# PSUM as eight one-bank tiles instead of three two-bank and two one-bank tiles, with sums of products taken bank by bank

## The chip, the core and the metric

One core of a Trainium2 chip. The metric is device time in microseconds (us) of one execution. A core has a matrix engine (PE; its weight loads are listed apart as PEld), three engines for elementwise work (DVE, ACT, POOL) and a queue that issues most transfers (SP). Each works through its own instruction list in order, and they hand results to one another by semaphores. PSUM, into which PE writes its products, has eight banks of 512 fp32 columns on 128 partitions; DVE and ACT read it, POOL and the transfers don't.

## The reference

Attention with a band mask over q, k, v of 8 batches x 8 heads x 576 positions x 64, half of the heads with a plain window of 32 and half with a dilated one; then a Fourier mixing, a normalisation and a two-layer perceptron with a residual:

```python
scores = scale * np.matmul(q, k.transpose(0, 1, 3, 2))
scores = np.where(masks[None, :, :, :], scores, -1000000000.0)
attn = softmax(scores)                       # max, exp, sum, divide
x = (attn @ v) as (B, S, C)                  # C = 512
u = x + real(fft(fft(x, axis=1), axis=2))
un = (u - mean(u)) / sqrt(var(u) + 1e-6)
out = u + maximum(un @ w_ch1, 0.0) @ w_ch2   # 512 -> 2048 -> 512
```

## The kernel before

**Order.** No engine's list is written by hand. Each step is registered with `add(engine, cost, function, reads, writes, priority)`, and `Plan.run` (L238) places the steps on the engines by a list schedule over assumed costs, such as `dve(n)` (L354); the instructions are then emitted in that order, and the waits between engines are generated from what each instruction reads and writes. The planner knows its buffers by tag: a step that first touches a new buffer of a tag is placed only once the buffer that many slots back has been given up (`place`, L256). So the order is fixed before the program runs; the semaphores only hold an engine back at a place in its list.

**PSUM.** Three tiles `duo0` to `duo2` of 1024 columns (two banks each) and two tiles of one bank, `ff0` and `ff1` (L396 to L401). The halves of the duos serve different steps: both halves of `duo0` are the pair `sc` (scores), the halves of `duo1` are `pt` and `av`, those of `duo2` are the two slots of `mix`. In the last stage each duo is used whole, as an accumulator of 1024 columns.

**Attention** (L518 to L630, until about 509 us). 96 steps; in each, PE writes scores into a half of each bank of `sc` (L547), DVE adds the mask and takes the minimum (L556), ACT exponentiates (L562), PE transposes into `pt` (L575), ACT copies that out as `ptsb` (L578), PE multiplies with v into `av` (L582), and DVE reads `av` for the sums, the reciprocal and the scaled output `xt` (L590 to L594), which SP stores.

**Mixing** (L683 to L859), one batch after another beside attention: POOL, DVE and ACT fold the rows; PE transforms along the sequence (L764, L786) into the slots of `mix`, ACT and DVE copy that out in two parts (`y`, L769 and L770; `ye`, L791 and L792); PE transforms along the channels (L810, L816), again into `mix`, and ACT (`pc`, L820) and DVE (`dm`, `sq`, L824 and L826) read it. Then come normalisation and a store.

**Fills** (L1103 to L1127). Six of the sixteen feature blocks of the perceptron are done beside and behind mixing, in 18 fills of 256 tokens. A fill has six *ups* (L944: 12 matmuls of 256 columns into one bank, then ACT L950 and DVE L952 read that bank, one after the other) and, for each of two tiles, a *down* of 18 matmuls of 512 columns (L960) that ACT copies out as `row` (L980). Thirteen fills use `ff0` and `ff1` in turn; the five *late* ones use `pt` and `av` in turn for the ups and the halves of `sc` for the downs (L1105, L1110, L1114). Beside them weights for the last stage are loaded into the two buffers `wst` and prepared by ACT, DVE and POOL.

**Last stage** (L1197 to L1295, from about 752 us): nine chunks of 512 tokens, the other ten feature blocks. `late_up` (L1205) uses `ff`; `late_down` (L1241) computes seven products per pair of blocks into two accumulators, `ab` and `cd`, each a duo; POOL, ACT and DVE build the operands (L900, L902, L1223 to L1227). After the last pair `finish_two` (L1014) adds both accumulators to rows in SBUF with six DVE instructions (L1034), multiplies and adds once per tile (L1045), and stores. It is called 18 times.

Of the kernel before, what the change touches and what calls it, by code (L numbers as in the profile page):

```python
# [9 lines left out]
F32 = mybir.dt.float32  # L10
# [5 lines left out]
ALU = mybir.AluOpType  # L16

B, H, S, D = 8, 8, 576, 64
C, FF = 512, 2048
P = 128  # L20
# [5 lines left out]
TOK1 = 2 * P  # L26
# [153 lines left out]
class Plan:  # L180
# [21 lines left out]
    def add(self, eng, cost, fn, r=(), w=(), prio=0.0, nbytes=0, at=0.0):  # L202
        op = Op()
        op.eng, op.cost, op.fn, op.prio, op.nbytes = eng, cost, fn, prio, nbytes
        op.num, op.after, op.ready, op.start = len(self.ops), [], at, None
        self.ops.append(op)
        deps, bufs = set(), {}
        for items, writes in ((r, False), (w, True)):
            for it in items:
                b, key = it if isinstance(it, tuple) else (it, None)  # L210
                bufs[id(b)] = b
                keys = set(b.writer) | set(b.readers) if key is None else {key, None}
                for x in keys:
                    if x in b.writer:
                        deps.add(b.writer[x])
                    if writes:
                        deps.update(b.readers.get(x, ()))
        for items, writes in ((r, False), (w, True)):
            for it in items:
                b, key = it if isinstance(it, tuple) else (it, None)  # L220
                if writes:
                    if key is None:
                        b.writer, b.readers = {None: op.num}, {}
                    else:
                        b.writer[key] = op.num
                        b.readers.pop(key, None)
                else:
                    b.readers.setdefault(key, []).append(op.num)
        op.bufs = list(bufs.values())
        for b in op.bufs:  # L230
            b.left += 1
        deps.discard(op.num)
        op.waits = len(deps)
        for d in deps:
            self.ops[d].after.append(op)
        return op
# [109 lines left out]
def pe(n, m=P):  # L346
    return max(n / 2400 + 0.0025, m / 1200)
# [6 lines left out]
def dve(n):  # L354
    return n * 0.00104 + 0.07
# [17 lines left out]
def fused_kernel(ctx: ExitStack, tc, q, k, v, w1, w2, seq, tail, chn, alt, mask, ident, perm, flip, out):  # L373
    nc = tc.nc
    plan = Plan()
    add = plan.add
# [11 lines left out]
    pools = {}  # L388
# [4 lines left out]
    pools["mix"] = keep = mix_ctx.enter_context(tc.tile_pool(name="mix", bufs=1))  # L393
    pools["att"] = heads = att_ctx.enter_context(tc.tile_pool(name="att", bufs=1, side="right"))

    duos = [pools["psum"].tile([P, 1024], F32, name=f"duo{i}") for i in range(3)]  # L396
    zs = [pools["psum"].tile([P, 512], F32, name=f"ff{i}") for i in range(2)]
    pair, (pt_bank, av_bank), mixes = [[d[:, :512], d[:, 512:]] for d in duos]
    views = {"sc": pair, "pt": [pt_bank], "av": [av_bank], "mix": mixes, "ff": zs}
    views.update({f"duo{i}": [d] for i, d in enumerate(duos)})  # L400
    plan.behind.update({"sc": ("half",), "duo0": ("sc", "half"), "duo1": ("pt", "av"), "duo2": ("mix",)})  # L401

    def halves():
# [8 lines left out]
    def ring(tag, of):  # L412
        b = Buf(None, tag)
        plan.slots[tag] = len(of)
        line = plan.tags.setdefault(tag, [])
        ap = of[len(line) % len(of)]
        b.make = lambda: ap
        line.append(b)
        return b

    def bank(tag):
        return ring(tag, views[tag])
# [13 lines left out]
    def utb(i=0):  # L436
        return ffnb("ut", [P, 2, KT, TOK1], F32R, NUT)
# [33 lines left out]
    def dma(fn, r, w, prio, nbytes, slow=1):  # L471
        return add("SP", 0.5, fn, r, w, prio, nbytes * slow)
# [390 lines left out]
    def flat(t, lo, n, dtype=F32):  # L863
        return t().rearrange("p i k t -> p (i k t)")[:, lo:lo + n].bitcast(dtype)
# [118 lines left out]
    def read_u(idx, dst, key, prio):  # L983
        if order(idx) == 0:
            dma(lambda: nc.sync.dma_start(out=dst(), in_=u_rows(idx)), ((us[idx // 4], idx % 4),), (key,), prio, P * 2056)
        else:
            kk = order(idx) - 1
            add("POOL", 1.04, lambda: nc.gpsimd.indirect_dma_start(
                dst(), None, us[idx // 4](), bass.IndirectOffsetOnAxis(ap=flip_sb()[:, 4 * kk + idx % 4:4 * kk + idx % 4 + 1], axis=0)),
                ((us[idx // 4], idx % 4), flip_sb), (key,), prio, P * 2056)  # L990
        add("ACT", act(C), lambda: nc.scalar.activation(
            out=dst()[:, 0:C], in_=dst()[:, 0:C], func=AF.Identity, bias=dst()[:, C:C + 1], scale=1.0), (), (key,), prio)

    def write_out(idx, row, done, prio):
        if idx >= NREST:
            pair_ = idx - NREST
            queues = ((nc.sync, "SP"), (nc.scalar, "ACT"))
            for n in range(4):
                e, side = divmod(n, 2)

                def put(e=e, side=side):
                    lo = 256 + 33 * side
                    p0 = 64 * e + 32 * side
                    queues[e][0].dma_start(out=out[2 * pair_ + e, lo:lo + 32], in_=row()[p0:p0 + 32])
                add(queues[e][1], 0.5, put, (done,), (), prio, 32 * 2048)
            return
        for b, lo, p0, n in out_rows(idx):
            dma(lambda b=b, lo=lo, p0=p0, n=n: nc.sync.dma_start(
                out=out[b, lo:lo + n], in_=row()[p0:p0 + n]), (done,), (), prio, n * 2048)

    def blocks(x):
        return x.rearrange("p (n c) -> p n c", c=TOK1)

    def finish_two(idx, ab, cd, prio):  # L1014

        f1, f2 = utb(), utb()
        uks = [(f2, ("u", e)) for e in range(2)]

        def u(e):
            return flat(f2, (C + 2) * e, C + 2)  # L1020

        def part():
            return flat(f1, 0, 2 * C)

        for e in range(2):
            read_u(idx + e, lambda e=e: u(e), uks[e], prio)
            dma(lambda e=e: nc.sync.dma_start(out=part()[:, C * e:C * e + C], in_=parts[idx + e]()),
                (parts[idx + e],), ((f1, ("p", e)),), prio, P * 2048)
        ps = ((f1, ("p", 0)), (f1, ("p", 1)))
        soon = min(prio, SOON)  # L1030
        outer, inner = slice(0, 4, 3), slice(1, 3)

        def take(at, x, need, op=ALU.add):
            add("DVE", dve(C), lambda: nc.vector.tensor_tensor(  # L1034
                out=blocks(part())[:, at], in0=blocks(part())[:, at], in1=x(), op=op), need, ps, soon)
        take(outer, lambda: blocks(ab())[:, 3::-3], (ab,))
        take(inner, lambda: blocks(ab())[:, 0:2], (ab,))
        take(outer, lambda: blocks(ab())[:, 2:0:-1], (ab,), ALU.subtract)
        take(inner, lambda: blocks(ab())[:, 2:4], (ab,))
        take(outer, lambda: blocks(cd())[:, 2:4], ((cd, 1),))  # L1040
        take(outer, lambda: blocks(cd())[:, 0:1].broadcast_to([P, 2, TOK1]), ((cd, 0),))
        for e in range(2):
            def row(e=e):
                return part()[:, C * e:C * e + C]
            add("DVE", dve(C), lambda e=e, row=row: nc.vector.scalar_tensor_tensor(  # L1045
                row(), row(), u(e)[:, C + 1:C + 2], u(e)[:, 0:C], op0=ALU.mult, op1=ALU.add), (uks[e],), (ps[e],), soon)
            write_out(idx + e, row, ps[e], prio)
# [43 lines left out]
    def load_ut(c, gate, prio):  # L1091
        raw, tr = utb(), utb()
        ut = ring("utl", utviews)
        tokens(c, 0, 4, (raw, lambda: words(raw)), (tr, lambda: words(tr)), ut, 1, "POOL", (gate,), min(prio, SOON))
        return ut
# [47 lines left out]
    w2s = [Buf() for _ in range(NPAIR)]  # L1143
# [91 lines left out]
    def late_down(p, hl, accs2, prio):  # L1235
        for n, (i, j, which, block, opens) in enumerate(PRODUCTS):
            acc = accs2[which]

            def go(i=i, j=j, block=block, opens=opens, acc=acc):
                for n, (a, x) in enumerate(PASSES):  # L1240
                    nc.tensor.matmul(  # L1241
                        acc()[:, TOK1 * block:TOK1 * block + TOK1], lhsT=hl()[:, a, i], rhs=w2s[p]()[:, j, x],
                        start=(opens and p == 0 and n == 0), stop=(p == NPAIR - 1 and n == 2), skip_group_check=True,
                    )
            key = (hl, ("raw" if i < 2 else "sum", 0)), (hl, ("raw" if i < 2 else "sum", 1))
            add("PE", 3 * pe(TOK1), go, (*key, w2s[p]), ((acc, block // 2),), prio + 0.001 * n)
# [76 lines left out]
```

## Time and profile before

| | |
|---|---|
| three timed runs | 1256.28, 1256.88, 1265.43 us (median 1256.88) |
| the profiled execution | 1251.71 us, of which the span from the first to the last instruction is 1249.9 us |
| PE busy | 1133.9 us (91%) |
| PEld busy | 984.5 us (79%) |
| DVE, ACT, POOL busy | 743.2, 524.6, 518.0 us |
| mean granted clock of PE | 0.981 of full |

In the rows below an engine's idle time stands in brackets or behind a bar with what ended it (`<-ACT low L950`: an instruction of ACT at line 950 that wrote `low`). Matmuls overlap and their ends are modelled, so a stall looks longer on PEld, whose loads are short, than on PE; the two are views of one stall and are not added. In the names of the trace `duo` stands for any of the three duos.

### The profile page before, as it was taken

Reading aid. Unit: us, or ns where it says so; the run is one execution under the profiler, and the core shown is the slowest. Engines: PE = TensorE matmul, PEld = TensorE weight load, DVE = VectorE, ACT = ScalarE, POOL = GpSimd, SP = SyncE. Lnnn points to the kernel's source line nnn. Section 1 sums busy time; section 2 is a strip of 40 time slices with the busy share of each in tenths; the row PEclk is TensorE's granted clock in tenths of the full one; section 3 lists DMA queues with packets and bytes.
Section 4 is the critical chain, followed back from the end, with each engine's and each line's share of the span. In section 5 each row is a group of like instructions: output and inputs, shape, how many; then the busy total and the mean of one; then the engine's idle time right before and its main releaser. Section 6 shows DMA issues by size and latency. Waiting matters only on the chain.

```text
span 1249.9 us, 21610 instructions
## 1 busy us (share of the span) xinstructions
PE 1133.9 (91%) x7750; PEld 984.5 (79%) x7750; DVE 743.2 (59%) x2141; ACT 524.6 (42%) x1282; POOL 518.0 (41%) x636
## 2 busy tenths in 40 slices
PE   8998878889889888989987779999999999999996
PEld 7886767677778777868866668888898988889886
DVE  6577857665556654778645324547384654738446
ACT  5456635544544543343423114433334343343432
POOL 2034534434224221563321115737456373655644
PEclk9899989999798999999999999999999999999999
DMA  9464527444435431524423222222240422314121
GB/s 318 151 199 158 176 62 210 129 149 123 138 106 168 119 111 54 155 85 144 135 84 101 51 72 81 59 78 68 77 126 19 118 68 68 86 59 127 34 86 34
DMA packets 103805, 137.14 MB, mean 110 GB/s; under 512 B 9145, under 2 KB 61817, under 8 KB 103697
## 3 DMA queue, kind: packets, MB, share of 16 engines
q1 hardware_dynamic: 100128, 126.85, 34.2%
q0 software_dynamic: 3040, 8.09, 2.2%
q8 instruction: 61, 1.00, 0.3%
q10 hardware_dynamic: 528, 0.82, 0.2%
q14 instruction: 48, 0.39, 0.1%
HBM read 97.92 MB, written 37.80 MB: 109 GB/s over the span
## 4 chain that ended last, share of the span: by engine, by line
PE 55%; DVE 7%; ACT 4%; issue 3%; POOL 1%; DVEq 0%; ACTq 0%; POOLq 0%
PE ff L1205 19%; PE duo L1241 15%; PE ff L944 5%; PE ff L960 4%; PE duo L944 4%; PE duo L960 2%; DVE low L902 2%; ACT low L1084 2%; PE duo L810 1%; PE duo L582 1%; PE duo L547 1%; DVE low L952 1%; ACT low L950 1%; PE duo L764 1%; PE duo L575 1%
## 5 line engine op out<-in xcount | busy, mean ns | idle before, releaser
L1205 PE MATMUL ff<-low,wb 128*128 128x512 f32 x1080 | 263.5, 394 | 0.0
L1205 PEld LDWEIGHTS ff<-low,wb 128*128 128x128 f32 x1080 | 197.2, 188 | 42.2 <-POOL low L1087 3.4
L562 ACT ACTIVATE pm<-pm,mx 96x128 f32<-96x128 f32 x384 | 131.9, 394 | 74.3 <-DVE mx L556 73.1
L1241 PE MATMUL duo<-w2s,low 128*128 128x256 f32 x1134 | 148.9, 283 | 5.0 <-DVE low L902 5.0
L1241 PEld LDWEIGHTS duo<-w2s,low 128*128 128x128 f32 x1134 | 143.9, 190 | 11.6 <-DVE low L902 7.2
L902 DVE TENSOR_TENSOR low<-y,low 128x640 fp32r<-128x640 f32 x90 | 86.7, 963 | 82.6 <-ACT low L900 82.6
L944 PE MATMUL ff<-ut,low 128*128 128x256 f32 x936 | 132.2, 292 | 2.3 <-DVE low L952 1.3
L900 ACT CAST low<-y 128x640 fp32r<-128x640 f32 x90 | 65.5, 728 | 157.2 <-POOL y L1227 119.2
L944 PEld LDWEIGHTS ff<-ut,low 128*128 128x128 f32 x936 | 120.3, 195 | 4.1 <-DVE low L952 1.7
L556 DVE CUSTOM_DVE_ANT_0 pm<-duo,mask_sb 96x128 f32<-96x128 f32 x384 | 92.7, 279 | 41.8 <-PE duo L547 40.9
L960 PE MATMUL ff<-low 128*128 128x512 f32 x468 | 112.9, 393 | 0.5 <-DVE low L952 0.5
L902 DVE TENSOR_TENSOR low<-xa,low 128x256 fp32r<-128x256 f32 x45 | 36.5, 810 | 119.7 <-ACT low L900 119.7
L1241 PE MATMUL duo<-low 128*128 128x256 f32 x756 | 98.7, 284 | 2.4 <-DVE low L902 2.3
L1241 PEld LDWEIGHTS duo<-low 128*128 128x128 f32 x756 | 94.7, 191 | 7.2 <-DVE low L902 5.0
L960 PEld LDWEIGHTS ff<-low 128*128 128x128 f32 x468 | 85.8, 188 | 17.4 <-DVE low L952 0.7
L582 PE MATMUL duo<-vt,ptsb 128*96 128x65 f32 x768 | 90.4, 259 | 9.0 <-DVE xt L594 5.1
L582 PEld LDWEIGHTS duo<-vt,ptsb 128*96 128x96 f32 x768 | 81.5, 174 | 19.6 <-DVE xt L594 9.7
L1223 POOL TENSOR_TENSOR y<-xa 128x256 f32<-128x256 f32 x45 | 33.3, 739 | 150.3 <-ACT xa L1211 144.8
L1211 ACT ACTIVATE xa<-ff 128x256 f32<-128x256 f32 x90 | 34.5, 384 | 124.2 <-PE ff L1205 120.9
L944 PE MATMUL duo<-ut,low 128*128 128x256 f32 x360 | 55.7, 294 | 24.5 <-DVE low L952 12.5
L1067 DVE STREAM_TRANSPOSE ut<-ut 128x512 f32<-128x512 f32 (+1 forms) x76 | 70.5, 968 | 11.2 <-DMA ut<-us 10.7
L547 PE MATMUL duo<-kb,tq 64*96 64x128 f32 x768 | 66.7, 302 | 7.8 <-DVE mx L556 7.3
(136 smaller groups left out, 1955.2 us busy)
## 6 DMA issues: line engine op xcount, KB each, us to landing
vt<-in_v_dram SPq DMA_DIRECT2D x32, 390.0 KB
wst<-in_w_dram SPq DMA_DIRECT2D x20, 512.0 KB
us<-uc SPq DMA_DIRECT2D x36, 257.0 KB
tq<-in_q_dram SPq DMA_DIRECT2D x32, 288.0 KB
part<-row SPq DMA_DIRECT2D x36, 256.0 KB
ut<-us SPq DMA_DIRECT2D x36, 256.0 KB
ut<-part SPq DMA_DIRECT2D x36, 256.0 KB
kb<-in_k_dram SPq DMA_DIRECT2D x31, 288.0 KB
```

The source lines that it names most:

```text
L547: nc.tensor.matmul(sc()[e][:QB, KB * n:KB * n + KB], lhsT=tq()[ps, QB * t:QB * t + QB], rhs=kb()[ps, QB * t:QB * t + KB], start=True, stop ...
L556: nc.vector.tensor_tensor_reduce(pm()[:, i], sc()[i % 2][:QB, KB * (i // 2):KB * (i // 2) + KB], mask_sb()[:, masks[blocks[i // 2]]], -0.1 ...
L562: add("ACT", 0.295, lambda i=i: nc.scalar.activation(out=pm()[:, i], in_=pm()[:, i], func=AF.Exp, bias=mx()[:, i:i + 1], scale=-1.0), ((mx ...
L582: add("PE", 0.16, lambda i=i: nc.tensor.matmul(av()[:QB, 65 * i:65 * i + 65], lhsT=pt()[:, i], rhs=vt()[:, i % 2, blocks[i // 2]], start=T ...
L900: add("ACT", act(n), lambda: nc.scalar.copy(out=dst(0), in_=src()), need, ((key[0], (key[1], 0)),), prio)
L902: add(eng, (pool if eng == "POOL" else dve)(n), lambda: lo.tensor_tensor(out=dst(1), in0=src(), in1=dst(0).bitcast(F32), op=ALU.subtract), ...
L944: nc.tensor.matmul(z()[:, :n_tok], lhsT=wf()[:, a, kk], rhs=ut()[:, p, kk], start=(kk == 0 and n == 0), stop=(kk == KT - 1 and n == 2),)
L960: nc.tensor.matmul(acc(), lhsT=h()[:, a, P * s:P * s + P], rhs=wf()[:, p], start=(first and n == 0), stop=(last and n == 2),)
L1067: nc.vector.transpose(out=o[back], in_=x[:, g])
L1205: nc.tensor.matmul(z(), lhsT=wb1[NF1 + 2 * p + f]()[:, a, kk], rhs=ut()[:, x, kk], start=(kk == 0 and n == 0), stop=(kk == KT - 1 and n == 2),
L1211: add("ACT", act(TOK1) - 0.05, lambda z=z, x=x, side=side, cols=cols: nc.scalar.activation(out=x()[:, cols], in_=z()[:, TOK1 * side:TOK1 * ...
L1241: nc.tensor.matmul(acc()[:, TOK1 * block:TOK1 * block + TOK1], lhsT=hl()[:, a, i], rhs=w2s[p]()[:, j, x], start=(opens and p == 0 and n == ...
```

## The change

Eight tiles `bank0` to `bank7` of one bank each take the place of the duos and of `ff`, in the same places. `sc`, `pt`, `av`, `mix` and `ff` name single banks as before. A buffer of a duo tag is now a list of two banks, made by a function (`callable(ap)`). `late_down` picks the bank by `block // 2`. In `finish_two` the four DVE instructions that read both halves of `ab` become six, three for each bank: one of 512 columns and two of 256; the two that read `cd` stay. The planner is told the smaller cost for the 256-column ones.

```diff
-    duos = [pools["psum"].tile([P, 1024], F32, name=f"duo{i}") for i in range(3)]
-    zs = [pools["psum"].tile([P, 512], F32, name=f"ff{i}") for i in range(2)]
-    pair, (pt_bank, av_bank), mixes = [[d[:, :512], d[:, 512:]] for d in duos]
-    views = {"sc": pair, "pt": [pt_bank], "av": [av_bank], "mix": mixes, "ff": zs}
-    views.update({f"duo{i}": [d] for i, d in enumerate(duos)})
+    eight = [pools["psum"].tile([P, 512], F32, name=f"bank{i}") for i in range(8)]
+    pair, pt_av, mixes, zs = [eight[i:i + 2] for i in range(0, 8, 2)]
+    views = {"sc": pair, "pt": pt_av[:1], "av": pt_av[1:], "mix": mixes, "ff": zs}
+    views.update({f"duo{i}": [lambda i=i: eight[2 * i:2 * i + 2]] for i in range(3)})
...
-        b.make = lambda: ap
+        b.make = ap if callable(ap) else lambda: ap
...
         def take(at, x, need, op=ALU.add):
-            add("DVE", dve(C), lambda: nc.vector.tensor_tensor(
+            add("DVE", dve(C if at in (outer, inner) else TOK1), lambda: nc.vector.tensor_tensor(
                 out=blocks(part())[:, at], in0=blocks(part())[:, at], in1=x(), op=op), need, ps, soon)
-        take(outer, lambda: blocks(ab())[:, 3::-3], (ab,))
-        take(inner, lambda: blocks(ab())[:, 0:2], (ab,))
-        take(outer, lambda: blocks(ab())[:, 2:0:-1], (ab,), ALU.subtract)
-        take(inner, lambda: blocks(ab())[:, 2:4], (ab,))
-        take(outer, lambda: blocks(cd())[:, 2:4], ((cd, 1),))
-        take(outer, lambda: blocks(cd())[:, 0:1].broadcast_to([P, 2, TOK1]), ((cd, 0),))
+        for n in range(2):
+            take(inner, lambda n=n: blocks(ab()[n]), ((ab, n),))
+            take(slice(3 * (1 - n), 3 * (1 - n) + 1), lambda n=n: blocks(ab()[n])[:, n:n + 1], ((ab, n),))
+            take(slice(3 * (1 - n), 3 * (1 - n) + 1), lambda n=n: blocks(ab()[n])[:, 1 - n:2 - n], ((ab, n),), ALU.subtract)
+        take(outer, lambda: blocks(cd()[1]), ((cd, 1),))
+        take(outer, lambda: blocks(cd()[0])[:, 0:1].broadcast_to([P, 2, TOK1]), ((cd, 0),))
...
-                        acc()[:, TOK1 * block:TOK1 * block + TOK1], lhsT=hl()[:, a, i], rhs=w2s[p]()[:, j, x],
+                        acc()[block // 2][:, TOK1 * (block % 2):TOK1 * (block % 2) + TOK1], lhsT=hl()[:, a, i], rhs=w2s[p]()[:, j, x],
```

## Rows read from the trace of the kernel before

**Rows 1.** The page, part 2: busy tenths of PE and its granted clock in 40 slices of 31.2 us.
```profile
PE   8998878889889888989987779999999999999996
...
PEclk9899989999798999999999999999999999999999
```
**Rows 2.** Busy time of the engines by stage: attention with mixing and the first fills, late fills, last stage, its end. Columns: stretch and its length, PE, PEld, DVE, ACT, POOL busy us with instructions, granted clock, DMA share, GB/s.
```profile
0.00:628.00 628.00, 555.41 (x4247) 478.31 (x4248) 411.94 (x1697) 299.67 (x783) 221.28 (x288) 0.96 0.48 144
628.00:752.00 124.00, 95.97 (x534) 77.58 (x533) 45.22 (x77) 29.61 (x62) 21.41 (x20) 1.00 0.28 80
752.00:1220.00 468.00, 462.80 (x2823) 410.25 (x2823) 266.71 (x340) 188.33 (x423) 260.56 (x310) 1.00 0.27 76
1220.00:1250.00 30.00, 19.68 (x151) 18.37 (x149) 19.33 (x28) 6.95 (x14) 14.71 (x18) 0.95 0.13 36
```
**Rows 3.** Waits of PEld from 0 to 628 us: who waited for whom, us in total, times, longest.
```profile
PEld duo L575 <- ACT pm L562: 13.8, 28, 1.2
PEld duo L547 <- DVE mx L556: 12.7, 24, 0.9
PEld duo L582 <- DVE xt L594: 9.7, 20, 1.6
PEld duo L575 <- DVE sums L590: 8.9, 18, 1.0
PEld duo L575 <- DVE xt L594: 8.8, 13, 1.2
PEld duo L810 <- ACT pc L820: 7.2, 15, 0.8
PEld duo L764 <- DVE y L770: 5.4, 6, 1.1
PEld duo L582 <- ACT ptsb L578: 5.0, 11, 0.8
PEld duo L786 <- DVE y L770: 4.8, 7, 1.0
...
PEld duo L764 <- ACT ye L791: 3.6, 5, 0.7
...
PEld duo L810 <- DVE dm L824: 2.5, 3, 0.9
PEld duo L764 <- ACT y L769: 2.4, 6, 0.5
PEld duo L816 <- DVE sq L826: 2.4, 3, 0.8
```
**Rows 4.** Waits of DVE and of ACT from 0 to 628 us, those between a reader of one half of `duo1` and a user of the other half.
```profile
DVE sums L590 <- PE duo L575: 18.0, 26, 2.6
...
DVE sums L590 <- ACT ptsb L578: 7.6, 13, 1.2
...
ACT ptsb L578 <- DVE sums L590: 18.6, 17, 4.0
...
ACT ptsb L578 <- PE duo L582: 8.6, 7, 2.6
```
**Rows 5.** The timeline in a late fill: start us, us, engine, line, operation, count, and the idle time before it with what ended it.
```profile
731.91 0.42 PEld L944 LDWEIGHTS duo<-ut,low 128*128 128x128 f32 x3 [0.68 <-ACT low L950]
...
732.64 0.42 DVE L952 SCALAR_TENSOR_TENSOR low<-duo,low 128x256 fp32r<-128x256 f32 x1 [2.58 <-PE duo L944]
733.12 1.13 PEld L944 LDWEIGHTS duo<-ut,low 128*128 128x128 f32 x9 [0.79 <-DVE low L952]
...
734.55 0.38 ACT L950 ACTIVATE low<-duo 128x256 fp32r<-128x256 f32 x1 [2.69 <-PE duo L944]
734.99 0.42 PEld L944 LDWEIGHTS duo<-ut,low 128*128 128x128 f32 x3 [0.74 <-ACT low L950]
```
**Rows 6.** Waits of PEld from 628 to 752 us, all there are.
```profile
PEld duo L944 <- ACT low L950: 17.2, 24, 1.2
PEld duo L944 <- DVE low L952: 17.0, 21, 1.2
PEld duo L960 <- ACT row L980: 5.6, 5, 1.1
```
**Rows 7.** PE's matmuls of the late fills by line, 628 to 752 us: count, busy us, mean ns, and idle us before them.
```profile
L944 PE MATMUL duo<-ut,low 128*128 128x256 f32 x354 | 54.6, 294 | 24.5 <-DVE low L952 12.5 <-ACT low L950 12.1
L960 PE MATMUL duo<-low 128*128 128x512 f32 x179 | 43.4, 394 | 3.5 <-ACT row L980 3.5
```
**Rows 8.** The chain of work that ended last, two pieces of a fill in `ff`: start us, us, what, matmuls.
```profile
613.88 2.84 PE ff L944 x24
...
619.97 8.17 PE ff L960 x36
```
**Rows 9.** The queue's own waits (SP) over the span: loads of `wst` behind POOL's preparation.
```profile
SPq L882 <- POOL wb L902: 34.8, 10, 6.0
```
**Rows 10.** A window of 6 us, with the columns of rows 2.
```profile
324.00:330.00 6.00, 5.35 (x33) 4.43 (x33) 2.74 (x19) 3.48 (x10) 0.00 (x0) 0.50 0.52 146
```
**Rows 11.** DVE's instructions that read a duo: duration ns min/median/max, first and last start us, shapes.
```profile
L1034 DVE TENSOR_TENSOR ut<-ut,duo x108: 672/679/691, 799.5 to 1243.9; 128x512 f32<-128x512 f32 x108
...
L824 DVE TENSOR_TENSOR dm<-pc,duo x24: 389/418/426, 110.7 to 576.4; 128x258 f32<-128x258 f32 x16, 33x258 f32<-33x258 f32 x8
```
**Rows 12.** Waits of PEld in the last stage, 752 to 1220 us, for DVE.
```profile
PEld duo L1241 <- DVE low L902: 9.4, 16, 0.7
```

## The prediction

> **What bounds the kernel now.** I read the busy line by slices first: PE is at 9 in every slice of the last 40% except the final one, and at 7 to 9 before that, so whatever this change gives must come from the first 750 us [rows 1]. The windows by stage say how much room there is: 72.6 us without PE work in the first 628 us (628 - 555.4), 28.0 in the late fills (124 - 96.0), 5.2 in the 468 us of the last stage [rows 2]. No other engine is full in the first two: DVE has 66% and 36%.
>
> Next, the waits, to see whom PE stalls for. In the late fills three rows hold all of it, 39.8 us on PEld [rows 6]. The timeline shows the pattern: PE starts an up in one half of `duo1` the moment ACT has read the *other* half, does three matmuls, stands still until DVE has read that other half too, then does nine. ACT and DVE in turn start only when PE has paused [rows 5]. These instructions share no column and no bank with one another, only the tile. The same in attention: DVE's `sums` reads `av` and waits 18.0 us for transposes into `pt`; ACT's `ptsb` reads `pt` and waits 18.6 us for `sums`; neither needs the other's data [rows 4]. So the generated waits order engines by tile, also a reader against a reader, and a tile of two banks ties two unrelated steps together.
>
> **Late fills.** The change makes `pt` and `av`, and the halves of `sc`, tiles of their own. All of [rows 6] is then without a cause: the up waits for the other bank, and the down of one tile (L960) for the copy of the other tile's bank. What it leaves can be read from the earlier fills, which do the same instructions on two one-bank tiles: 24 matmuls of an up in 2.84 us, 36 of a down in 8.17 us, that is 0.118 and 0.227 us each [rows 8]. The stage holds 354 and 179 of them [rows 7]: 354 x 0.118 + 179 x 0.227 = 82.5 us, against 124: a gain of 41.5. One up now takes 734.99 - 731.91 = 3.08 us [rows 5]; at the other rate it is 1.42, in which ACT (0.38) and DVE (0.42) can empty the other bank. From below: in the second and third late fill the weights are prepared too, and their loads already wait for POOL to free `wst` [rows 9]; DVE's list mixes that preparation with L952, so a late load holds L952, and behind it the next up but one. Those waits are 3.5 us each (34.8 / 10); if four loads are late by that and PE with them, the gain is 41.5 - 14 = 27.5. I take 36, nearer to the upper end, because [rows 6] gives 39.8 by another view, and DVE's work of this stage fits (45 us in what becomes 85 to 90).
>
> **The first 628 us.** I sort PEld's waits [rows 3] by what the instruction needs. Nine rows are waits for the reader of another bank: transposes into `pt` for readers of `av` (8.9 + 8.8), and the transforms in one slot of `mix` for readers of the other slot (7.2, 2.5, 5.4, 2.4, 3.6, 4.8, 2.4): 46.0 us. They lose their cause. Four rows are true: L575 needs the exponentials `pm` (13.8), L547 the half of `sc` that DVE reads (12.7), L582 the one bank `av` (9.7) and `ptsb` (5.0): 41.2 us. But three of these are late because ACT and DVE were themselves held by the other half [rows 4]: `sums`, and with it `xt`, by 25.6 us, `ptsb` by 27.2 us, and the exponentials behind `ptsb` in ACT's list.
>
> Of the 46.0 I take 70%, 32 us: where a false wait goes, the next true one on PE's fixed list comes nearer, and DVE, which will have 412 us of work in some 570 instead of 628, answers later. Of the 28.5 us for `pm`, `xt` and `ptsb` two thirds, 19. Of `mx` a quarter, 3: the change splits `sc` between its two banks, so DVE can start on the first bank one matmul earlier, but two steps still share each bank, in halves of 256 columns, and the new scores wait for the old. [...]
>
> [...] I take a fifth back, 5 us; bounds 0 and 25. Sum here: 32 + 19 + 3 + 5 = 59 us. Bounds: 15, a third of the 46.0 with nothing else, and 46 + 41 + 25 = 112, everything.
>
> **Last stage.** In each of 18 `finish_two` DVE has two instructions more: four of 512 columns at 0.679 us were 2.72; two of these and four of 256 at 0.418 (the nearest row, 258 columns read from PSUM) are 3.03 [rows 11]. That is 0.31 us each, 5.7 in all. The cover is DVE's idle time, 201 of the 468 us [rows 2]; PE's only waits for DVE here are for L902, 9.4 us in 16 [rows 12]. If every added 0.31 held L902, it would be 5.7 us. I take 0, and 0.3 for the last `finish_two`, behind which there is no work. `cd` can be read one product earlier, which the six takes of `ab` before it hide. The first `take` starts at 799.5 us [rows 11], so the planner, whose costs differ only there, places everything before as now. The views, the function in `ring` and the names add no instruction; no transfer is added or moved, and SP's stores and loads only follow their producers earlier.
>
> **Sum:** 36 + 59 - 0 = 95 us. The profiled execution took 1251.7 us, so 1157; the median of the runs is 5 above it, so 1162 by that. I say **1158 us**.
>
> **Rivals.**
> *The next wait takes over.* PE's list is fixed; a step freed from `av` may only stand until `pm` or the loads arrive. Then the first stage gives 15 and the late fills 27.5: 1256.9 - 42.5 = 1214. For it: DVE at 66%, and mixing is a chain over four engines. Against it: [rows 4] lie on that very chain.
> *Everything behind follows.* 41 and some 95 of the 112: 1256.9 - 136 = 1121. For it: the waits of ACT and DVE in [rows 4] sum to 53 us beside PE's own, and stalls shorter than a matmul's modelled end don't show. Against it: DVE would have to run at 412 of about 530 us. [...]
> *The waits don't go.* If the releasers named in [rows 4, 6] stood for other semaphores, nothing is released: 1257, no change. Against it: the pattern repeats with the same 0.68 and 0.79 us at every up.
> *Slower: the split sums.* DVE works in order; if the added 0.31 us stand ahead of L902 in each of 18 places, PE stands 5.7 us, and the end is 0.3 later: 1263. It decides only if the first two stages give less than 6 us. Against it: 57% DVE.
>
> **How the numbers follow.** Forecast (1130 to 1190) 0.60; next wait 0.17; everything follows 0.16; no release 0.04; split sums 0.03. A change under 1%, 12.6 us, can't be told from none in this kernel. The first three cases are faster by more than that, 0.93; the fourth and a third of the fifth lie within 1%, 0.05; slower by more 0.02, where the split sums cost more than reckoned. The range takes in the forecast and most of both neighbours: 1112 to 1208.
>
> **What would show it.** Right: from the late fills L944 and L960 at 0.118 and 0.227 us each, the stage near 85 to 90 us, and no wait of PE for L950 within an up; in attention no wait of `sums` for L575 nor of `ptsb` for `sums`; more DVE share in the first stage; the 468 us of the last stage unchanged. Wrong in size: waits of L575 for `pm` or of L952 for transfers that grow by as much as the others fall. Wrong in kind: the pairs of [rows 4] still there between different banks.

## The result and the profile after

The changed kernel takes **1138.34 us** (median of 4 runs, 1136.03 to 1143.46); the kernel before, run beside it, 1256.58. The ratio is 0.9063, with a 95% interval of 0.8995 to 0.9131. The forecast was 1158 us, with a range of 1112 to 1208.

Medians and means below leave out the runs that took over 1.5% longer than the fastest of their kernel: two of E1's ten (1266.73 and 1269.13 us), one of E8's six (1495.78) and one of the eleven of the kernel before that ran beside E5 to E8 (1611.23).

The profiled execution of the changed kernel is the slowest of its four, 1143.46 us, and that of before was 5 us faster than its median. So the traces show 108.2 us of the 118. The page's head and the slices of PE answer to [rows 1]; line numbers from L547 on are one lower than before.

```profile
span 1141.7 us, 21571 instructions
...
PE 1097.8 (96%) x7750; PEld 976.1 (85%) x7750; DVE 737.1 (65%) x2177; ACT 520.6 (46%) x1282; POOL 516.2 (45%) x636
...
PE   9999999999999999999999999999999999999996
...
PEclk9998999999989999999999999999999999999998
```

PE is now at 9 in every slice but the last. The windows by stage answer to [rows 2]: attention with mixing, late fills, last stage, its end; the columns are the same.

```profile
0.00:557.90 557.90, 531.90 (x4248) 472.47 (x4249) 410.76 (x1698) 295.06 (x783) 220.83 (x288) 0.98 0.53 162
557.90:643.10 85.20, 83.64 (x536) 75.69 (x535) 45.34 (x77) 29.54 (x62) 22.01 (x20) 1.00 0.42 116
643.10:1111.10 468.00, 462.84 (x2824) 409.88 (x2823) 262.01 (x372) 189.08 (x423) 258.92 (x310) 1.00 0.27 76
1111.10:1142.00 30.90, 19.43 (x149) 18.05 (x147) 19.04 (x32) 6.95 (x14) 14.46 (x18) 0.90 0.12 35
```

The first stage fell from 628.0 to 557.9 us (-70.1, forecast -59), the late fills from 124.0 to 85.2 (-38.8, forecast -36); the 468.0 us of the last stage are the same to the tenth; the rest of the span grew from 29.9 to 30.6 us. Together -108.2, forecast -95. DVE's, ACT's and POOL's busy times hardly change. Of PE, 72.1 us of idle time are gone (116.0 to 43.9 of the span) and 36.1 us of busy time. Of the latter, 12.3 fall in the late fills, where the clock is 1.00 in both: a matmul of L944 that lasted 294 ns on average there beside stalls lasts 282 in an unbroken row. The other 23.5 are in the first stage, where the clock rose too, from 0.96 to 0.98.

Waits of PEld in the first stage, the counterpart of [rows 3] (us in total, times, longest):

```profile
PEld bank L546 <- DVE mx L555: 10.8, 22, 1.0
PEld bank L581 <- DVE xt L593: 7.4, 12, 1.6
PEld bank L574 <- ACT pm L561: 6.8, 19, 0.6
PEld bank L763 <- POOL eot L734: 2.9, 3, 1.5
PEld bank L574 <- ACT ptsb L577: 2.9, 11, 0.6
```

Of the nine rows that the prediction called false eight are gone; of the ninth (L786 for `y`, 4.8 us, here L785) 1.2 us are left. Three of the four true ones are still there, and a small one, 0.7 us before, has grown: the transposes wait for ACT to empty `pt` (2.9). Waits of DVE and ACT in the same stretch, the counterpart of [rows 4]:

```profile
DVE sums L589 <- PE bank L581: 23.4, 21, 5.2
...
ACT ptsb L577 <- PE bank L574: 21.1, 29, 2.0
...
ACT ptsb L577 <- PE bank L581: 12.1, 5, 4.0
```

`sums` now waits only for the matmuls into `av` that it reads. The last line answers to the 8.6 us of [rows 4] and has not gone: `ptsb` has three buffers, L581 (L582 before) reads them, and ACT waits its turn. That row was a true dependence and was read wrongly as false.

In the late fills one wait of PEld is left, against three rows and 39.8 us [rows 6]:

```profile
PEld bank L943 <- DVE low L951: 2.4, 3, 1.7
```

The chain of waits has long unbroken pieces there (start us, us, what, matmuls):

```profile
601.52 8.19 PE bank L959 x36
609.71 8.52 PE bank L943 x72
```

That is 0.227 us for each of a down and 0.118 for each of an up, as taken from [rows 8].

At the end, the timeline shows what the split of the sums costs (start us, us, engine, line, operation, count, idle before). The kernel before:

```profile
1240.82 3.80 DVE L1034 TENSOR_TENSOR ut<-ut,duo 128x512 f32<-128x512 f32 x6 [1.56 <-PE duo L1241]
```

The changed kernel:

```profile
1121.94 2.32 PEld L1240 LDWEIGHTS bank<-w2s,low 128*128 128x128 f32 x19 [0.73 <-DVE ut L1033]
...
1131.91 4.44 DVE L1033 TENSOR_TENSOR ut<-ut,bank 128x512 f32<-128x512 f32 x8 [1.26 <-PE bank L1240]
```

Eight instructions take 4.44 us, where six took 3.80: 0.64 more, not 0.31. The eight by shape (count, busy us, mean ns, idle before):

```profile
L1033 DVE TENSOR_TENSOR ut<-ut,bank 128x512 f32<-128x512 f32 x4 | 2.7, 686 | 1.5 <-PE bank L1240 1.3
L1033 DVE TENSOR_TENSOR ut<-ut,bank 128x256 f32<-128x256 f32 x4 | 1.7, 416 | 0.1
```

Their durations add up to 4.41 us, those of the six (681 ns each) to 4.09: 0.32 more, as priced. The rest is overlap. Before, most of these instructions start 0.60 us after the one in front, though each lasts 0.68; only one of the six, which adds to columns that the one in front has just written, starts 0.71 us after it, 0.03 us behind its end. In the new order four of the eight add to such columns, and start 0.03 to 0.10 us behind the end of the one in front. And PE waits 0.73 us for L1033, because `late_down` writes the second bank of `ab` first and `finish_two` empties it last. Both are only at the end: between 643 and 1111 us the length has not changed.

### The profile page after: what moved, and what is told of

It is laid out like the page before. It is cut to its first block, busy times and chain, and to the rows that moved or that the text cites. A ratio compares the mean times of both kernels' runs of the same rounds, so it can differ in the third digit from the quotient of the medians.

```text
span 1141.7 us, 21571 instructions
## 1 busy us (share of the span) xinstructions
PE 1097.8 (96%) x7750; PEld 976.1 (85%) x7750; DVE 737.1 (65%) x2177; ACT 520.6 (46%) x1282; POOL 516.2 (45%) x636
## 4 chain that ended last, share of the span: by engine, by line
PE 74%; DVE 13%; ACT 4%; issue 3%; POOL 2%; DMA 2%; SPq 0%; DVEq 0%; POOLq 0%; ACTq 0%
PE bank L1204 21%; PE bank L1240 17%; PE bank L943 10%; PE bank L959 9%; PE bank L581 4%; PE bank L546 4%; PE bank L809 2%; PE bank L574 2%; DVE low L901 2%; DVE pm L555 2%; PE bank L763 2%; PE bank L492 2%; ACT low L1083 2%; ACT pm L561 1%; DMA tq<-in_q_dram 1%
## 5 line engine op out<-in xcount | busy, mean ns | idle before, releaser
L1204 PE MATMUL bank<-low,wb 128*128 128x512 f32 x1080 | 264.9, 394 | 0.0
L1204 PEld LDWEIGHTS bank<-low,wb 128*128 128x128 f32 x1080 | 196.4, 188 | 41.8 <-POOL low L1086 3.5
L943 PE MATMUL bank<-ut,low 128*128 128x256 f32 x1296 | 176.5, 289 | 4.3 <-DVE low L951 3.2
L943 PEld LDWEIGHTS bank<-ut,low 128*128 128x128 f32 x1296 | 163.7, 193 | 8.0 <-DVE low L951 5.0
L1240 PEld LDWEIGHTS bank<-w2s,low 128*128 128x128 f32 x1134 | 144.9, 189 | 12.8 <-DVE low L901 6.7
L959 PE MATMUL bank<-low 128*128 128x512 f32 x648 | 155.0, 392 | 0.5 <-DVE low L951 0.5
L1240 PE MATMUL bank<-w2s,low 128*128 128x256 f32 x1134 | 150.1, 282 | 5.2 <-DVE low L901 4.7
L959 PEld LDWEIGHTS bank<-low 128*128 128x128 f32 x648 | 119.1, 188 | 24.1 <-DVE low L951 0.7
L901 DVE TENSOR_TENSOR low<-y,low 128x640 fp32r<-128x640 f32 x90 | 83.4, 927 | 86.3 <-ACT low L899 86.3
L899 ACT CAST low<-y 128x640 fp32r<-128x640 f32 x90 | 65.6, 729 | 153.1 <-POOL y L1226 118.8
L555 DVE CUSTOM_DVE_ANT_0 pm<-bank,mask_sb 96x128 f32<-96x128 f32 x384 | 92.6, 279 | 38.7 <-PE bank L546 37.1
L901 DVE TENSOR_TENSOR low<-xa,low 128x256 fp32r<-128x256 f32 x45 | 33.4, 743 | 119.6 <-ACT low L899 119.6
L1240 PE MATMUL bank<-low 128*128 128x256 f32 x756 | 98.7, 284 | 2.4 <-DVE low L901 2.3
L1240 PEld LDWEIGHTS bank<-low 128*128 128x128 f32 x756 | 94.7, 191 | 7.2 <-DVE low L901 5.0
L581 PE MATMUL bank<-vt,ptsb 128*96 128x65 f32 x768 | 85.7, 252 | 4.9 <-DVE xt L593 4.9
L581 PEld LDWEIGHTS bank<-vt,ptsb 128*96 128x96 f32 x768 | 78.0, 168 | 13.0 <-DVE xt L593 7.4
L1033 DVE TENSOR_TENSOR ut<-ut,bank 128x512 f32<-128x512 f32 (+1 forms) x144 | 75.3, 548 | 4.6 <-PE bank L1240 1.3
L1066 DVE STREAM_TRANSPOSE ut<-ut 128x512 f32<-128x512 f32 (+1 forms) x76 | 70.8, 977 | 11.2 <-DMA ut<-us 11.1
```

The costliest lines, as they stand in the source:

```text
L555: nc.vector.tensor_tensor_reduce(pm()[:, i], sc()[i % 2][:QB, KB * (i // 2):KB * (i // 2) + KB], mask_sb()[:, masks[blocks[i // 2]]], -0.1 ...
L581: add("PE", 0.16, lambda i=i: nc.tensor.matmul(av()[:QB, 65 * i:65 * i + 65], lhsT=pt()[:, i], rhs=vt()[:, i % 2, blocks[i // 2]], start=T ...
L899: add("ACT", act(n), lambda: nc.scalar.copy(out=dst(0), in_=src()), need, ((key[0], (key[1], 0)),), prio)
L901: add(eng, (pool if eng == "POOL" else dve)(n), lambda: lo.tensor_tensor(out=dst(1), in0=src(), in1=dst(0).bitcast(F32), op=ALU.subtract), ...
L943: nc.tensor.matmul(z()[:, :n_tok], lhsT=wf()[:, a, kk], rhs=ut()[:, p, kk], start=(kk == 0 and n == 0), stop=(kk == KT - 1 and n == 2),)
L959: nc.tensor.matmul(acc(), lhsT=h()[:, a, P * s:P * s + P], rhs=wf()[:, p], start=(first and n == 0), stop=(last and n == 2),)
```

## The experiments

In kernels with the function edited in E1, lines stand five higher than before (L575 is L580); in the others they are those of after. Times are medians; "late fills" and "first stage" are lengths from the trace. Each kernel has the added sums; E1 to E4 and E8 differ only in which pairs of banks are tiles of their own.

**E1: all the new code, but three two-bank tiles.** The eight banks are halves of duos again, except `ff`:

```diff
-    eight = [pools["psum"].tile([P, 512], F32, name=f"bank{i}") for i in range(8)]
+    eight = []
+    for i in range(4):
+        if i in (3,):
+            eight += [pools["psum"].tile([P, 512], F32, name=f"bank{2 * i + h}") for h in range(2)]
+        else:
+            t = pools["psum"].tile([P, 1024], F32, name=f"duo{i}")
+            eight += [t[:, :512], t[:, 512:]]
```

> The changed kernel with its bank-by-bank sums, but with the three two-bank tiles of before under the same views, so that only the waits of the tiles come back. If the gain comes from the waits between banks of one tile: back to the time of before, 1256 us, plus at most the 5.7 us of the added sums, of which I expect about 1 us at the end; ratio to before 1.000 to 1.005, and the waits of rows 4 and 6 are there again. If the gain came from the sums or from another order of the instructions: 1140 to 1200 us, with those waits or without.

Measured: 1253.63 us, ratio 0.9976 (0.9931 to 1.0021); first stage 626.4, late fills 124.2. The waits of PEld in the late fills, all there are, answer to [rows 6]:

```profile
PEld duo L949 <- ACT low L955: 17.2, 24, 1.2
PEld duo L949 <- DVE low L957: 17.0, 21, 1.2
PEld duo L965 <- ACT row L985: 5.6, 5, 1.1
```

In the first stage the two leading pairs of [rows 4] are back as well:

```profile
DVE sums L595 <- PE duo L580: 17.9, 24, 2.6
...
ACT ptsb L583 <- DVE sums L595: 17.5, 16, 4.0
```

The same addresses and the same instructions as the changed kernel, the waits of before, and nothing gained: what gives the gain is the declaration of the tile, and the added sums cost nothing that can be measured.

**E2: `pt` and `av` apart.**

```diff
-        if i in (3,):
+        if i in (1, 3):
```

> Only the tile of pt and av is split; the pair of the scores and the mixing slots keep their two-bank tiles. By the sorted waits: in the late fills the 34.2 us of L944 go and the 5.6 us of L960 stay; in attention the 17.7 us of transposes behind readers of av go, with most of the 19 us reckoned for exponentials, xt and ptsb: 34 + 35 = 69 us less than before, 1188 us. If the next wait takes over once mixing still stalls: late fills 34 and attention under 15, about 1208 us.

Measured: 1184.83 us, ratio 0.9424 (0.9363 to 0.9485); first stage 595.4 (-31.0 against E1), late fills 89.3 (-34.9). In the late fills the 34.2 us for which the ups waited [rows 6] are down to 1.5; the 5.6 for `row`, which belong to `sc`, are still there. PEld's instructions by line, first stage (count, busy us, mean ns, idle before them and its releasers), first of E1, then of E2:

```profile
L580 PEld LDWEIGHTS duo<-ident_sb,pm 96*128 96x128 f32 x192 | 22.3, 153 | 19.0 <-ACT pm L567 8.3 <-DVE sums L595 3.8 <-DVE xt L599 3.7
L580 PEld LDWEIGHTS duo<-perm_sb,pm 96*128 96x128 f32 x192 | 22.0, 150 | 18.1 <-DVE sums L595 5.6 <-DVE xt L599 5.3 <-ACT pm L567 5.0
```

The same lines of E2:

```profile
L580 PEld LDWEIGHTS bank<-ident_sb,pm 96*128 96x128 f32 x192 | 21.6, 149 | 8.4 <-ACT pm L567 3.9 <-ACT ptsb L583 2.7
L580 PEld LDWEIGHTS bank<-perm_sb,pm 96*128 96x128 f32 x192 | 20.9, 146 | 5.1 <-ACT pm L567 2.7 <-ACT ptsb L583 0.8
```

`sums` and `xt` are gone as releasers, and the wait for `pm` halves from 13.3 to 6.6 with them: ACT is itself on time. With the matmuls into `av` (L587, 19.7 to 14.6) that is 28.7 us less idle time. The stage's clock differs too, 0.973 in E1 and 0.980 in E2, which by an estimate (626.4 x 0.027 - 595.4 x 0.020) is 5 of the 31.0.

**E3: `mix` apart.**

```diff
-        if i in (3,):
+        if i in (2, 3):
```

> Only the tile of the two mixing slots is split. By the sorted waits the 28.3 us listed for L764, L786, L810 and L816, of which 70% to all: 20 to 28 us less than before, 1228 to 1236 us, all of it in the first stage, the late fills as before (124 us). If mixing was hidden behind the stalls of attention and only follows when those go: under 10 us, about 1248 us.

Measured: 1217.84 us, ratio 0.9654 (0.9589 to 0.9719), better than expected. First stage 585.8, late fills 133.5, the latter longer than in E1 though nothing of theirs is changed: their granted clock is 0.90, not 1.00.

**E4: the halves of `sc` apart.**

```diff
-        if i in (3,):
+        if i in (0, 3):
```

> Only the tile of the pair of the scores is split. The late fills lose the 5.6 us of L960; in attention a quarter of the 12.7 us of L547 behind mx: 3 us. Together 8 to 9 us less than before, 1248 us. If the masks on DVE, which can start one bank earlier, speed up the whole chain of attention: 20 us or more, under 1237 us.

Measured: 1259.01 us (10 runs), ratio 0.9985 (0.995 to 1.0021): no gain that can be told, against an expected 9. The wait for `row` is gone in the late fills, but they take 128.0 us at a clock of 0.91.

**E5: the second bank taken first.**

```diff
-        for n in range(2):
+        for n in (1, 0):
```

> The changed kernel, but finish_two empties the second bank of ab before the first. In the changed kernel PE waits 0.73 us near the end for L1033 on the second bank, which is written again first, and the eight takes after the last matmul last 4.44 us, of which the first bank's product is the last to come. If these two are what the bank-by-bank sums cost: no wait of L1240 for L1033, takes starting about 0.3 us earlier against the last matmul, the last stage 0.7 to 1.1 us shorter, the total 1 us less than the changed kernel and not to be told from it. If the order matters in each of the 18 places: 5 us or more.

Measured: 1140.1 us (1138.33 to 1144.56), ratio 0.9101 (0.9067 to 0.9134), against 1136.41 for the changed kernel on the same chip (E7). The intervals overlap, and the mean clocks are 0.991 and 0.994: no gain, and no loss that can be told. PEld's idle time before the matmuls of L1240 that read `w2s` and `low`, of E5:

```profile
L1240 PEld LDWEIGHTS bank<-w2s,low 128*128 128x128 f32 x1134 | 144.8, 189 | 13.3 <-DVE low L901 7.7 <-ACT low L899 0.4
```

and of E7:

```profile
L1240 PEld LDWEIGHTS bank<-w2s,low 128*128 128x128 f32 x1134 | 144.9, 189 | 12.8 <-DVE low L901 6.8 <-DVE ut L1033 0.7
```

The 0.7 us for L1033 went, and the waits for L901 (0.9) and L899 (0.4) grew by more: the operands of the next matmuls were not ready any earlier.

**E6: the masks bank by bank.** In the three loops of `attend` over the four quarters of `sc`:

```diff
-        for i in range(4):
+        for i in (0, 2, 1, 3):
```

> The changed kernel, but masks, exponentials and transposes of a step go in the order 0, 2, 1, 3, so that DVE reads the first bank of sc twice and then the second, where it alternated. The largest wait left is L546 for mx, 10.8 us in 22. If PE waits there for the bank it writes first: that bank is free one mask (0.28 us) earlier, 22 x 0.28 = up to 6 us less than the changed kernel, about 1132 us. If it waits for the last mask whatever the order, because the next scores write both banks at once, or the next wait takes over: within 2 us of the changed kernel.

Measured: 1136.92 us, ratio 0.9069 (0.9036 to 0.9101), the same as E7. `mx` still holds PEld for 11.2 us. By the trace's records the matmuls into the first bank wait 8.5 us instead of E7's 9.5, and those into the second, which come right behind, 2.7 instead of 1.6.

**E7: the changed kernel again.**

> The changed kernel itself, for comparison on the same chip: 0.906 of before, 1138 us.

Measured: 1136.41 us, ratio 0.9065 (0.9033 to 0.9097); first stage 553.4, late fills 85.3.

**E8: all apart but `sc`.**

```diff
-        if i in (3,):
+        if i in (1, 2, 3):
```

> The tiles of pt and av and of the mixing slots split, the pair of the scores not. The pair alone gave nothing that could be told (0.9985 of before). If it gives nothing here either: the time of the changed kernel, 1138 us. If its share only shows once the other stalls are gone: L960 behind L980 5.6 us, and L547 behind mx 15.1 us as with pt and av alone against 10.8 with all split: 6 to 10 us more than the changed kernel, 1144 to 1148 us.

Measured: 1143.81 us, ratio 0.9129 (0.9092 to 0.9166). Once the other pairs are apart, `sc` is worth 7.4 us by the medians; 4.0 of them are the late fills (89.3 to 85.3), where the 5.6 for `row` stands. The windows of the first stage, of E8 and of E7:

```profile
0.00:552.60 552.60, 522.49 (x4248) 462.64 (x4249) 410.20 (x1698) 294.76 (x783) 221.55 (x288) 1.00 0.54 164
0.00:553.40 553.40, 527.76 (x4247) 467.64 (x4248) 409.58 (x1698) 295.36 (x783) 221.20 (x288) 0.99 0.53 164
```

The lengths are the same only because E8's profile had the higher clock: PE is idle for 30.1 us in E8 and 25.6 in E7, and PEld waits 15.5 and 11.1 us for `mx`.

**E9, E10, E11: E4, E3 and E1 again, one execution each**, for the clock of the late fills.

> A second profile of the kernel with only the pair of the scores split. In the first its late fills ran at a granted clock of 0.91 and took 128 us, though the 5.6 us of L960 were gone; over ten runs its mean clock was 0.968 against 0.977 with no tile split. If the late fills with shorter stalls regularly meet the lower clock: again below 0.95 there and 125 us or more. If the first profile was chance: 1.00 and 118 to 120 us.

> A second profile of the kernel with only the mixing slots split; its first had late fills at 0.90 and 133.5 us. Chance: 1.00 and 124 us, as with no tile split. Regular: below 0.95 and 130 us or more. The first stage in either case 0.98 to 0.99 and 584 to 592 us.

> A second profile of the kernel with no tile split and bank-by-bank sums; the first had late fills at 1.00 and 124.2 us, and the first stage at 0.97 and 626 us. If the clock of the late fills belongs to the kernel: 1.00 and 124 us again. If it is chance from run to run: it may fall here as it did in the other two.

Measured: 1257.46, 1217.41 and 1272.81 us; the late fills 126.0 (clock 0.93), 128.8 (0.95) and 131.3 (0.92). E9 came out as its "regular" case had it, E10 between its two, and E11 shows that the kernel of E1 has long late fills too. The windows of this stage, first of E1:

```profile
626.40:750.60 124.20, 96.17 (x535) 77.68 (x534) 45.13 (x76) 29.58 (x62) 21.40 (x20) 1.00 0.28 81
```

and of E11, the same kernel:

```profile
641.10:772.40 131.30, 103.25 (x536) 84.05 (x535) 45.08 (x77) 29.59 (x62) 21.40 (x20) 0.92 0.27 76
```

DVE's, ACT's and POOL's work is the same; PE is 7.1 us longer busy with the same matmuls. It is the clock, and it differs between runs of one kernel. So E3's and E4's long late fills need not come from their edits. Whether E4's edit makes them more frequent is not shown: its ten runs have a mean clock of 0.968, E1's eight 0.980.

E10 also prices the mixing at an equal clock: E1 and E10 both have 0.97 in the first stage, which takes 626.4 and 588.3 us. PEld by line in E1, the transforms:

```profile
L815 PEld LDWEIGHTS duo<-chn,y 128*128 128x128 f32 (+1 forms) x288 | 37.4, 171 | 14.8 <-ACT pc L825 7.2 <-DVE dm L829 2.5 <-DVE y L775 1.7
...
L769 PEld LDWEIGHTS duo<-seq,oos 128*128 128x128 f32 x96 | 14.3, 193 | 10.9 <-DVE y L775 4.6 <-ACT ye L796 3.6 <-ACT y L774 2.4
L769 PEld LDWEIGHTS duo<-tail_sb,eot 128*128 128x128 f32 x48 | 8.0, 198 | 8.3 <-issue 4.3 <-POOL eot L740 2.9 <-DVE y L775 0.9
L821 PEld LDWEIGHTS duo<-alt_sb,ye 128*128 128x128 f32 (+1 forms) x24 | 4.0, 167 | 5.6 <-DVE sq L831 2.4 <-DVE y L775 1.7 <-ACT y L774 1.4
...
L791 PEld LDWEIGHTS duo<-seq,ees 128*2 128x2 f32 x32 | 2.1, 84 | 5.6 <-DVE y L775 4.8
```

The same lines in E10:

```profile
L815 PEld LDWEIGHTS bank<-chn,y 128*128 128x128 f32 (+1 forms) x288 | 36.1, 165 | 2.8 <-DVE y L775 0.6 <-issue 0.3
...
L769 PEld LDWEIGHTS bank<-seq,oos 128*128 128x128 f32 x96 | 13.8, 190 | 1.0 <-DVE ye L797 0.6
L769 PEld LDWEIGHTS bank<-tail_sb,eot 128*128 128x128 f32 x48 | 8.1, 202 | 3.1 <-POOL eot L740 2.9
L821 PEld LDWEIGHTS bank<-alt_sb,ye 128*128 128x128 f32 (+1 forms) x24 | 4.0, 165 | 0.0
...
L791 PEld LDWEIGHTS bank<-seq,ees 128*2 128x2 f32 x32 | 2.4, 86 | 2.3 <-DVE y L775 0.9
```

Without the rows left out, idle time here falls from 45.2 (14.8 + 10.9 + 8.3 + 5.6 + 5.6) to 9.2 us, by 36.0, and the stage by 38.1; the 2.9 for `eot`, which the transform needs, stay.

None of the variants beats the changed kernel by more than can be measured.

## Why the prediction was right, and where it was off

**The mechanism was right.** A wait between two engines that only share a two-bank tile goes with the tile (E1 against E7), and each pair of banks gives back its own: -68.8, -35.8 and +5.4 us by the medians of E2, E3 and E4 against E1, together -99.2, against -117.2 for all at once (E7, on another chip). At one clock the third is a gain too (last section).

**Late fills: 36 taken, 38.8 measured.** The two rates held within 0.3%. The lower bound had the weights' preparation hold PE for 14 us; it holds it for 2.4.

**First stage, `pt` and `av`: 31.4 taken, 31.0 measured (E2), but by errors that cancel.** That is luck. The taken sum was 70% of 17.7 (12.4) plus two thirds of 28.5 (19). In fact the 17.7 went whole. Of the 28.5, in E1 and E2, `pm` fell from 13.3 to 6.6 and `ptsb` from 4.8 to below what the view lists for L587, but `xt` only from 10.3 to 8.9, about 13 in all; and the wait for `ptsb` at L580 rose from 1.1 to 3.5, the one for `mx` from 13.2 to 15.1. That makes some 26, and the clock about 5 more.

**First stage, mixing: 19.8 taken, 38 measured.** This is the step that failed. "Of the 46.0 I take 70%" counted 28.3 us of listed waits for the transforms and took off 30% for the next wait coming nearer. Their idle time in all was 45 us. Besides the 28.3, and 2.9 for `eot`, some 11 us stood in the same view in rows that were left out, waits for `y` and `sq` of 0.7 to 1.7 us and 4.3 for which it names no releaser; the rest is in waits too short for it. And nothing took their place: in E10 no other line's idle time grew by more than 0.8 us (L949), all together by 1.8.

**`sc`: 3 taken in this stage, 3.4 to 4.5 measured** (the medians of E8 and E7 less their late fills; PE's idle time). From before to after, `mx` falls only from 12.7 to 10.8 us, since with the other stalls gone it would be 15.5 (E8). The rest stays: the new scores write both banks in turn, and what one bank's matmuls no longer wait (9.5 to 8.5 us), the other's do (1.6 to 2.7, E6). Two steps still share each bank as one tile, and the 10.8 us are left. No run took the semaphore away, so whether scores could be written beside a mask that reads the other half of the bank is not shown; that a quarter of the wait would go was the author's estimate.

**Clock: 5 taken, about 15 reckoned afterwards** (an estimate, see the last section). The 25 us, of which the 5 are a fifth, are by an estimate what a granted clock of 0.96 takes of 628 us (628 x 0.04) [rows 2], with stretches at 0.50 [rows 10]; the fifth itself was the author's estimate, and no run shows it. What the profiles show in its place is a first stage at 0.98 in the changed kernel, 0.99 in E5 and E7 and 1.00 in E6, half of the missing 0.04 or more: the fifth was too little. Of the 20 us between 1158 and 1138, the mixing explains 18, the late fills 3 and the clock 10, against 5 by which `pt` and `av` fell short without the clock: 26. The 6 in excess are not told apart: the parts come from different runs, and the clock is in the stages' lengths too.

**Last stage: 0 and 0.3 taken, 0 and 0.7 measured.** The added sums are covered by DVE's idle time until the end. The count and the durations of the instructions were right (0.31 priced, 0.32 measured); the sum of durations left out that they overlap, and that the new order loses this overlap at four places where it was lost at one. That makes 0.64 us.

**The rivals.** "The next wait takes over" (1214) fell with E10, and holds in attention for a small part: `ptsb` at L580 and what `xt` kept. "Everything behind follows" (1121) is nearer than it seemed: by the medians 1138 lies 17 us from it and 20 from the forecast; by the traces the 108.2 us gained are nearer to the forecast's 95 than to its 136. DVE runs 74% of the first stage (410.8 of 557.9), where 78% (412 of 530) had been held against it. "The waits don't go" fell with E1 and E7. "Slower: the split sums" fell with E1, which has them all and takes the time of before.

## What to carry to other kernels

Where waits are generated by tile, a PSUM tile should be no larger than what one step writes and one reader empties; here two unrelated steps in one tile ordered even a reader against a reader (18.6 us of ACT's `ptsb` behind DVE's `sums` [rows 4]), and with all pairs apart E7 takes 117.2 us less than E1. In the trace such a wait is known by a releaser that touches neither the columns nor the data of the waiting instruction, and by partners that wait for each other in turn. Price it by the idle time of all lines that write the tile, not by the longest rows of the list of waits.

## What the hardware showed that was not expected

**The clock moved the time from run to run, and hid small gains.** Eight runs of E1 lie between 1246.73 us at a mean granted clock of 0.988 and 1263.23 at 0.969, within 1.2 us of a line of 8.7 us for each 0.01; E4's ten runs have a slope of 8.5. Their means are 1253.9 us at 0.980 and 1258.6 at 0.968: at one clock E4 would be about 5 us faster than E1, near the 5.6 of the wait that it loses. By such a line, 850 us for the whole clock, before (mean 0.976) to E7 (0.994) holds 0.018 x 850 = 15 us of clock. The two chips differ no more than that: the kernel before took 1258.1 us at 0.974 beside E1 to E4 and 1253.3 at 0.980 beside E5 to E8.

The means of E2, E3 and E7 are 1186.1 us at 0.987, 1216.5 at 0.983 and 1137.0 at 0.994. Brought to 0.980 by this line, E2, E3 and E4 give -62, -35 and -5 us against E1, together about -103, and E7 -105: by this estimate the three parts just add.

**The same short stalls, with and without loss of clock.** Windows of E9's late fills, columns as above:

```profile
631.00:666.00 35.00, 27.10 (x161) 22.18 (x160) 13.88 (x25) 10.41 (x21) 8.78 (x8) 1.00 0.27 83
666.00:701.00 35.00, 28.40 (x132) 23.97 (x132) 16.33 (x30) 9.69 (x20) 3.22 (x3) 0.76 0.29 86
701.00:757.00 56.00, 45.08 (x246) 37.05 (x246) 14.99 (x24) 9.60 (x21) 9.65 (x10) 1.00 0.28 70
```

Ups with one or two stalls each run through all three windows (15 stalls in 121 matmuls of L949, 10 in 91, 20 in 144), and only the middle one loses clock. Over the stage, seven profiles with `pt` and `av` in one tile (before, E1, E3, E4, E9 to E11) show 1.00, 1.00, 0.90, 0.91, 0.93, 0.95 and 0.92; the six with them apart (after, E2, E5 to E8) 1.00 each. So in this stage the clock was below 1.00 only in profiles that have these waits, of at most 1.5 us on PEld in E4 (0.91); but before and E1 have as many of them (45 for `low`, of at most 1.2 us) at 1.00. Why one run loses the clock and another of the same kernel does not stays open; no experiment here changed the clock alone.
